# Twenty loads of a fused attention and gated-unit kernel, each cut into a 120-row and an 8-row transfer

## The chip, the cores and the metric

The kernel runs on one core of one Trainium2 chip. The metric is the device time of one execution in microseconds (us). Before the change three runs gave a median of 178.63 us (178.54 to 179.7). A further execution was recorded by the hardware profiler, and all views of the profile come from that one.

The core has five engines that run their own instruction streams side by side: TensorE (PE, matmuls; its weight loads are listed as PEld), VectorE (DVE), ScalarE (ACT), GpSimd (POOL) and SyncE (SP). SP computes nothing here: it issues the transfers between the chip's memory (HBM) and the on-chip memory (SBUF), which sixteen DMA engines carry out.

## The reference

Block-wise causal attention over 8 batches and 8 heads (576 positions, head size 64, blocks of 64 positions), whose output, with the heads side by side, goes through a gated linear unit with a causal convolution of five taps. All inputs and the output are float32.

```python
def _attn_ref(q, k, v):
    scores = (1.0 / np.sqrt(D)) * np.matmul(q, k.transpose(0, 1, 3, 2))
    scores = np.where(block_i >= block_j, scores, -1000000000.0)      # blocks of 64
    attn = np.exp(scores - np.max(scores, axis=-1, keepdims=True))
    attn = attn / (np.sum(attn, axis=-1, keepdims=True) + 1e-09)
    return np.matmul(attn, v)

def _moe_ref(x, w_val, conv_w, w_out):                # x: [8, 576, 512]
    for k in range(5):
        gate_pre += conv_w[k][None, None, :] * xp[:, k:k + S, :]
    gate = 1.0 / (1.0 + np.exp(-gate_pre))
    return gate * (x @ w_val) @ w_out
```

## The kernel before

The order of all work is written out by hand. A string, `PLAN` (lines 12 to 116), lists some 900 steps as `name/arguments/engine/banks`. The loop at the end (line 711) walks through it and calls the function of each step, which appends its instructions to the stream of the named engine. Each engine then runs its own steps in that order, and waits only where data or a buffer requires it. So the order on SP is the order in which the `S` steps stand in the plan.

The attention works in units. A unit `u` (0 to 15) is half a batch: four heads. Its q and k arrive through `lq(u, h)` and `lk(u, h)`, each with two halves `h`, 32 loads of q and 32 of k in all. One such load (`load_qk`, line 263) fills 128 partitions ("rows") of a staging buffer with 576 float32 numbers each: 64 groups of nine positions for each of two heads. There are three staging buffers each for q and for k, so a load waits until the buffer's old content has been used. `cd(u, i)` (line 351) then casts a unit's q (`i` = 0) or k (`i` = 1), both halves at once, to float16, on POOL, DVE or ACT. For the first unit `cds` does so half by half. `Tt` (line 388) transposes the result on PE, `Te` copies it back to SBUF as `qkT`, and `S` (scores), `E` (exponential, ACT), `A` (times v), `Nr`/`Nm` (normalization, DVE) and `X`/`Xe` (transpose into `xt`) follow for each pair of heads. v comes by `lv` (line 279) in 64 loads of 128 rows and four pieces of 256 bytes each, and is cast by `cv`; the last 64 positions of each batch come by `lvt`.

The gated unit then takes runs of 464 columns of `xt`: `C` (convolution on PE), `CS` (tanh on ACT), `V` (times `w_val`), `Ve` (gate times value into `gv`, DVE, line 653), and then `O` (times `w_out`), `Oe` (copy out) and `Od` (line 682, store, issued by SP).

The two weight matrices are loaded once, by `lwv` (line 291) and `lwo` (line 296), two loads each. One load fills 128 rows with two pieces of 512 float32 numbers. They borrow the memory of `gv` and of the output buffers `osb` as staging, and are cast by `cwv` and `cwo`.

All of these loads and stores are issued on SP's queue. Nearly every issue there carries a completion counter out of a ring of eight, and an issue waits until the transfer that last used its counter, eight issues earlier, has landed in full. At most eight transfers are therefore under way at a time. The profile's lines for these instructions are L265 (q and k), L281 (v), L287 (end of v), L292 and L297 (weights) and L683 (stores). Line 253 is the copy helper for DVE and POOL, line 251 that for ACT, line 144 the matmul helper and line 148 the transpose helper.

Of the kernel before, what the change touches and what calls it, by code (L numbers as in the profile page):

```python
# [119 lines left out]
def kernel(  # L120
# [37 lines left out]
    def consts(n, shape, dt, tag):  # L158
        return [const(shape, dt, f"{tag}_{i}") for i in range(n)]
# [56 lines left out]
    qks = [consts(3, [128, 2, 576], fp32, f"{n}s") for n in "qk"]  # L216
# [17 lines left out]
    w_val_st = gv[0:128, 0:4096].bitcast(fp32).rearrange("p (f n) -> p f n", f=4)  # L234
# [3 lines left out]
    w_out_st = osb_all[0:128, 0:2048].rearrange("p (f n) -> p f n", f=4)  # L238
# [5 lines left out]
    def rot(tiles, i):  # L244
        return tiles[i % len(tiles)]

    DMA = {"S": nc.sync, "A": nc.scalar}
# [12 lines left out]
        return f  # L260


    def load_qk(i, u, h, eng):
        b, w = divmod(u, 2)
        DMA[eng].dma_start(  # L265
            out=rot(qks[i], u)[0:128, h],
            in_=(q, k)[i][b, 4 * w + h:4 * w + h + 3:2, 0:576, 0:64].rearrange(
                "x (p n) d -> p x (n d)", n=9))

    @op  # L270
    def lq(u, h, eng="S", bank=None):
        load_qk(0, u, h, eng)

    @op
    def lk(u, h, eng="S", bank=None):
        load_qk(1, u, h, eng)
# [12 lines left out]

    @op  # L290
    def lwv(f, eng="S", bank=None):
        DMA[eng].dma_start(out=w_val_st[0:128, 2 * f:2 * f + 2],  # L292
                           in_=moe_w_val[256 * f:256 * f + 256].rearrange("(f p) n -> p f n", p=128))

    @op
    def lwo(f, eng="S", bank=None):
        DMA[eng].dma_start(out=w_out_st[0:128, 2 * f:2 * f + 2],  # L297
                           in_=moe_w_out[256 * f:256 * f + 256].rearrange("(f p) n -> p f n", p=128))

    @op  # L300
    def lcv(eng="S", bank=None):
# [409 lines left out]
    for word in PLAN.split():  # L711
        name, args, eng, bank = (word.split("/") + [""])[0:4]
        a = [int(i) for i in args.split(".") if i]
# [51 lines left out]
```

## Time and profile before

| | |
|---|---|
| runs shown, median | 178.63 us (178.54 to 179.7) |
| the profiled execution, its own time | 177.31 us |
| its span, from the first to the last instruction | 175.5 us |
| mean granted TensorE clock over the span | 0.968 |
| VectorE busy | 121.6 us (69%) |
| ScalarE busy | 144.8 us (82%) |
| GpSimd busy | 70.9 us (40%) |
| read from HBM, written to it | 30.42 MB, 9.44 MB |
| q and k loads, 288 KB each | 64 |
| v loads, 128 KB each | 64 and 8 |
| weight loads, 512 KB each | 4 |
| stores of 256 KB | 35 |

Times in the profile are counted from the first instruction of the span. An engine counts as busy while an instruction of it runs; SP's issues do not count. The ends of matmuls are modelled, so a busy PE is not necessarily at its best rate. In rows of the timeline the last bracket names how long the engine had been idle and what ended that; "issue" there means that the engine was waiting for nothing that the profile records.

### The profile page before, as it was taken

To read this page: it belongs to the slowest core of one execution; us is meant where nothing else is said; L and a number is where in the kernel's file an instruction comes from. 1 tells how busy PE (TensorE), PEld (TensorE's weight loads), DVE (VectorE), ACT (ScalarE), POOL (GpSimd) and SP (SyncE) were. 2 spreads that over 40 slices of the span, in tenths; PEclk is the share of its full clock that TensorE was granted. 3 is DMA by queue.
4 is the path that set the end of the run, shared out by engine and by line. 5 is a ranking of instruction groups with operands and counts; after the bars stand their busy time and mean duration, and the time that the engine had idled before them with its cause. 6 is when DMAs were issued, how large, how long until landed. Compare 5 with 4: busy or idle time off the path is not lost.

```text
span 175.5 us, 8114 instructions
## 1 busy us (share of the span) xinstructions
PE 165.6 (94%) x3498; PEld 99.6 (57%) x3498; DVE 121.6 (69%) x247; ACT 144.8 (82%) x179; POOL 70.9 (40%) x146
## 2 busy tenths in 40 slices
PE   6799899899999899899999999999999999999991
PEld 1456566456756465567556755665556665664540
DVE  2547998588769683999756998976698685545420
ACT  3799999889999699789889679988898878954562
POOL 5121875772552631486533643174546440100000
PEclk9855999999999999999999999999999999999998
DMA  4999899999999779998999969999987022103175
GB/s 141 306 364 280 234 241 392 327 232 252 238 301 262 132 185 287 334 292 241 311 327 246 304 197 259 290 302 222 322 253 213 4 97 86 63 4 120 38 296 209
DMA packets 53694, 40.38 MB, mean 230 GB/s; under 512 B 39701, under 2 KB 39957, under 8 KB 53658
## 3 DMA queue, kind: packets, MB, share of 16 engines
q1 hardware_dynamic: 53514, 39.74, 78.7%
q8 instruction: 27, 0.44, 1.1%
q10 hardware_dynamic: 144, 0.13, 0.2%
q14 instruction: 9, 0.07, 0.1%
HBM read 30.42 MB, written 9.44 MB: 227 GB/s over the span
## 4 chain that ended last, share of the span: by engine, by line
PE 80%; ACT 9%; DVE 3%; issue 3%; DMA 2%; SPq 0%; DVEq 0%; ACTq 0%
PE PS L144 72%; PE PS L148 8%; ACT pt L449 7%; DMA qs<-in_q_dram 2%; DVE gv L658 1%; ACT qkT L251 1%; DVE x L528 1%; DVE qkT L253 1%; DVE xt L253 0%; ACT q L251 0%; SPq L265 0%; ACT osb L251 0%; DVE rc L523 0%; ACT pt L488 0%; ACT late L251 0%
## 5 line engine op out<-in xcount | busy, mean ns | idle before, releaser
L449 ACT ACTIVATE pt<-PS 128x1024 f16<-128x1024 f32 (+1 forms) x102 | 93.8, 988 | 10.4 <-PE PS L144 8.8
L144 PE MATMUL PS<-qkT 64*128 64x64 f16 (+4 forms) x512 | 39.7, 257 | 2.3 <-issue 0.8
L144 PE MATMUL PS<-w_out,gv 128*128 128x512 f16 (+1 forms) x148 | 35.7, 374 | 0.2 <-DVE x L528 0.2
L144 PE MATMUL PS<-xt,w_val 128*128 128x464 f16 x160 | 35.7, 360 | 0.0
L658 DVE SCALAR_TENSOR_TENSOR gv<-th,PS 128x112 f16<-128x112 f32 (+4 forms) x64 | 26.2, 450 | 12.3 <-PE PS L144 6.0
L253 DVE COPY qkT<-PS 128x1152 f16<-128x1152 f16 (+1 forms) x22 | 29.1, 1326 | 8.1 <-PE PS L148 4.0
L144 PEld LDWEIGHTS <-pt 128*128 128x128 f16 (+1 forms) x960 | 27.9, 102 | 6.5 <-issue 1.8
L144 PE MATMUL PS<-v,pt 128*128 128x65 f16 (+1 forms) x896 | 31.1, 194 | 0.2 <-issue 0.2
L144 PEld LDWEIGHTS <-qkT 64*128 64x128 f16 x512 | 17.7, 96 | 18.6 <-issue 14.2
L640 ACT ACTIVATE th<-PS 128x928 f32<-128x928 f32 x20 | 17.8, 941 | 7.2 <-PE PS L144 7.1
L528 DVE TENSOR_TENSOR x<-PS,rc 128x512 f16<-128x512 f32 x32 | 22.1, 691 | 1.0
L144 PEld LDWEIGHTS <-w_val 128*128 128x128 f16 x160 | 13.9, 97 | 15.2 <-issue 3.6
L499 POOL MEMSET pt<- 64x256 f16 x32 | 10.9, 345 | 27.7 <-ACT pt L449 27.3
L144 PEld LDWEIGHTS <-gv 128*128 128x128 f16 x148 | 12.6, 97 | 13.5 <-issue 2.2
L253 POOL CAST k<-ks 128x1152 f16<-128x1152 f32 x12 | 13.8, 1148 | 11.9 <-DMA ks<-in_k_dram 6.0
L253 POOL CAST q<-qs 128x1152 f16<-128x1152 f32 x11 | 12.6, 1147 | 12.9 <-PE PS L144 6.1
L253 POOL CAST v<-vs 128x512 f16<-128x512 f32 x24 | 14.6, 618 | 6.7 <-DMA vs<-in_v_dram 5.1
L494 POOL MEMSET pt<- 64x256 f16 x32 | 10.0, 313 | 17.3 <-ACT pt L449 16.5
L253 DVE COPY xt<-PS 128x512 f16<-128x512 f16 (+1 forms) x30 | 11.6, 397 | 4.5 <-ACT th L640 2.3
L251 ACT COPY qkT<-PS 128x1152 f16<-128x1152 f16 (+1 forms) x16 | 14.2, 908 | 0.4 <-PE PS L148 0.4
L144 PE MATMUL PS<-xt,DG 32*32 32x464 f16 x800 | 13.0, 358 | 0.8 <-issue 0.7
L253 DVE COPY osb<-PS 128x512 f32<-128x512 f32 x17 | 11.6, 687 | 2.4 <-PE PS L144 1.7
(57 smaller groups left out, 135.3 us busy)
## 6 DMA issues: line engine op xcount, KB each, us to landing
ks<-in_k_dram SPq DMA_DIRECT2D x32, 288.0 KB, 5.0
qs<-in_q_dram SPq DMA_DIRECT2D x32, 288.0 KB, 5.5
out_dram<-osb SPq DMA_DIRECT2D x35, 256.0 KB, 4.3
vs<-in_v_dram SPq DMA_DIRECT2D x64, 128.0 KB, 5.1
vts<-in_v_dram SPq DMA_DIRECT2D x8, 128.0 KB, 5.0
osb<-in_moe_w_out_dram SPq DMA_DIRECT2D x2, 512.0 KB, 4.6
gv<-in_moe_w_val_dram SPq DMA_DIRECT2D x2, 512.0 KB, 5.7
out_dram<-late SPq DMA_DIRECT2D x1, 128.0 KB, 2.0
```

What stands on the lines that cost most here:

```text
L144: made.append(nc.tensor.matmul(out=out, lhsT=lhsT, rhs=rhs, start=start, stop=stop, skip_group_check=True))
L148: made.append(nc.tensor.transpose(out=out, in_=in_, identity=identity))
L251: i = nc.scalar.copy(out=out, in_=in_)
L253: i = (nc.vector if eng == "V" else nc.gpsimd).tensor_copy(out=out, in_=in_)
L449: made.append(nc.scalar.activation(out=o, in_=r, func=AF.Exp, bias=0.0, scale=0.125))
L494: nc.gpsimd.memset(rot(pts, p)[64:128, 0:2, 0:1024].rearrange("p h (t s) -> p h t s", t=2)[:, :, :, 0:64], 0.0)
L499: nc.gpsimd.memset(rot(pts, p)[64:128, 0:2, 640:1408].rearrange("p h (t s) -> p h t s", t=2)[:, :, :, 0:64], 0.0)
L528: made.append(nc.vector.tensor_tensor(out=rot(x16, p)[0:128].rearrange("p i h d -> p h i d"), in0=r[:, :, :, 0:64], in1=rot(rcs, p)[0:128] ...
L640: made.append(nc.scalar.activation(out=rot(ths, n)[0:128, 2 * i:2 * i + 2], in_=both(take("C", n, i))[:, :, 0:RUN], func=AF.Tanh, bias=0.0 ...
L658: made.append(nc.vector.scalar_tensor_tensor(out=gv[0:128, x, a - 4 * i:e - 4 * i], in0=rot(ths, n)[0:128, x, a - o:e - o], scalar=1.0, in ...
```

## The change

Twenty loads are each issued as two transfers, one of the first 120 rows and one of the last 8, one behind the other on the same queue. These are the four weight loads and sixteen of the 64 loads of q and k: q(1, 1), k(1, 1), k(2, 1) and q(3, 0), and then one of the four of each unit from 4 to 15 (k for odd units, q for even ones; half 0 for units 4, 5, 8, 9, 12, 13, half 1 for the others). The source and the destination of every byte stay as they are, and so do the plan and all instructions on the other four engines. SP issues twenty transfers more, and each of the twenty takes a counter of the ring of eight.

```diff
+    PARTED = {(0, 1, 1), (1, 1, 1), (1, 2, 1), (0, 3, 0)} | {(u % 2, u, u // 2 % 2) for u in range(4, 16)}
+
     def load_qk(i, u, h, eng):
         b, w = divmod(u, 2)
-        DMA[eng].dma_start(
-            out=rot(qks[i], u)[0:128, h],
-            in_=(q, k)[i][b, 4 * w + h:4 * w + h + 3:2, 0:576, 0:64].rearrange(
-                "x (p n) d -> p x (n d)", n=9))
+        src = (q, k)[i][b, 4 * w + h:4 * w + h + 3:2, 0:576, 0:64].rearrange(
+            "x (p n) d -> p x (n d)", n=9)
+        cuts = (0, 60, 64) if (i, u, h) in PARTED else (0, 64)
+        for a, e in zip(cuts, cuts[1:]):
+            DMA[eng].dma_start(out=rot(qks[i], u)[2 * a:2 * e, h], in_=src[a:e])
...
     def lwv(f, eng="S", bank=None):
-        DMA[eng].dma_start(out=w_val_st[0:128, 2 * f:2 * f + 2],
-                           in_=moe_w_val[256 * f:256 * f + 256].rearrange("(f p) n -> p f n", p=128))
+        src = moe_w_val[256 * f:256 * f + 256].rearrange("(f p) n -> p f n", p=128)
+        for rows in (slice(0, 120), slice(120, 128)):
+            DMA[eng].dma_start(out=w_val_st[rows, 2 * f:2 * f + 2], in_=src[rows])
```

`lwo` changes as `lwv` does, with `w_out_st` and `moe_w_out`.

More of the change, by code (lines that the diff above doesn't have):

```diff
@@ L291, in lwv @@
     def lwv(f, eng="S", bank=None):
-        DMA[eng].dma_start(out=w_val_st[0:128, 2 * f:2 * f + 2],
-                           in_=moe_w_val[256 * f:256 * f + 256].rearrange("(f p) n -> p f n", p=128))
+        src = moe_w_val[256 * f:256 * f + 256].rearrange("(f p) n -> p f n", p=128)
+        for rows in (slice(0, 120), slice(120, 128)):
+            DMA[eng].dma_start(out=w_val_st[rows, 2 * f:2 * f + 2], in_=src[rows])
     @op
     def lwo(f, eng="S", bank=None):
-        DMA[eng].dma_start(out=w_out_st[0:128, 2 * f:2 * f + 2],
-                           in_=moe_w_out[256 * f:256 * f + 256].rearrange("(f p) n -> p f n", p=128))
+        src = moe_w_out[256 * f:256 * f + 256].rearrange("(f p) n -> p f n", p=128)
+        for rows in (slice(0, 120), slice(120, 128)):
+            DMA[eng].dma_start(out=w_out_st[rows, 2 * f:2 * f + 2], in_=src[rows])
     @op
```

## The prediction

> **What bounds the kernel now.** I read the first page, then a table of busy time by stretch, then the waits of PE, SP's own timeline, and the waits of the casts that consume the loads. The page first.
>
> ```profile
> span 175.5 us, 8114 instructions
> PE 165.6 (94%) x3498; PEld 99.6 (57%) x3498; DVE 121.6 (69%) x247; ACT 144.8 (82%) x179; POOL 70.9 (40%) x146
> ...
> q1 hardware_dynamic: 53514, 39.74, 78.7%
> q8 instruction: 27, 0.44, 1.1%
> ...
> PE 80%; ACT 9%; DVE 3%; issue 3%; DMA 2%; SPq 0%; DVEq 0%; ACTq 0%
> ```
>
> PE is busy 94% of the span and carries 80% of the chain that ended last. The table of four stretches (start and end, length, then each engine's busy time, the granted clock, the mean busy share of the sixteen DMA engines and GB/s) says where PE is not full.
>
> ```profile
> 0.00:25.00 25.00, 21.50 (x339) 12.38 (x339) 15.70 (x29) 20.80 (x32) 10.90 (x34) 0.80 0.89 259
> 25.00:76.00 51.00, 48.27 (x1144) 29.51 (x1141) 38.66 (x81) 46.08 (x53) 25.58 (x51) 1.00 0.98 269
> 76.00:131.00 55.00, 54.98 (x1270) 33.60 (x1268) 43.80 (x85) 48.09 (x56) 25.68 (x44) 1.00 0.97 274
> 131.00:175.50 44.50, 40.81 (x763) 24.08 (x762) 23.47 (x56) 29.80 (x41) 8.70 (x19) 0.99 0.33 115
> ```
>
> From 25 to 76 us PE is idle for 51.00 - 48.27 = 2.73 us; from 76 to 131 it is idle for 0.02. So faster loads can win about 2.7 us in the second stretch and next to nothing in the third, where they can only lose. The DMA engines are at 0.98 and 0.97 in both, so the loads run close to their own limit beside PE.
>
> Three pauses of PE in the second stretch have no data as their cause. The waits of PE sum them up, the timeline places them, and a table cut at the points where PE resumes counts what lies between.
>
> ```profile
> PE PS L144 <- issue: 1.7, 3, 0.8
> ...
> 31.25 0.62 PE L144 MATMUL PS<-xt,DG 32*32 32x464 f16 x32 [0.71 <-issue]
> ...
> 59.29 0.42 PE L144 MATMUL PS<-qkT 64*128 64x64 f16 x6 [0.81 <-issue]
> ...
> 64.80 0.39 PE L144 MATMUL PS<-v,pt 128*128 128x65 f16 x7 [0.15 <-issue]
> ...
> 31.25:59.29 28.04, 27.05 (x639) 16.58 (x640) 21.52 (x45) 25.03 (x29) 15.21 (x26) 1.00 1.02 256
> 59.29:64.80 5.51, 5.35 (x129) 3.14 (x128) 3.79 (x8) 5.19 (x6) 2.32 (x4) 1.00 0.69 156
> ```
>
> Between the first two resumptions PE ran 639 + 640 = 1279 instructions, between the next two 129 + 128 = 257: five times 256, and once. Queue q8 moved 0.44 MB in 27 packets, 16.3 KB each. Divided by PE's 3498 + 3498 instructions that is 63 bytes for one, or 256 instructions a packet. So q8 brings PE's own program in blocks of 256, and PE stood still three times (0.71 + 0.81 + 0.15 = 1.67 us) because a block came late. That program travels over the same DMA engines as the loads. One packet takes 1.1% x 16 x 175.5 / 27 = 1.14 us of one engine. In the second stretch PE runs 1144 + 1141 instructions, about nine blocks or 10.2 us. If one engine carries them all, it has 10 us of extra work in 51 us in which the sixteen are 0.98 busy on average, so it must be the last to finish most loads.
>
> **The change part by part.** First the cost: twenty more issues on SP. SP's timeline (start, length, count) and the spread of the issues' lengths (minimum, median, maximum in ns):
>
> ```profile
> 56.20 3.35 SPq L265 DMA_DIRECT2D qs<-in_q_dram  x1
> 59.65 2.19 SPq L281 DMA_DIRECT2D vs<-in_v_dram  x4
> 61.89 2.14 SPq L265 DMA_DIRECT2D ks<-in_k_dram  x1
> 64.12 0.54 SPq L281 DMA_DIRECT2D vs<-in_v_dram  x1
> 64.71 0.54 SPq L265 DMA_DIRECT2D qs<-in_q_dram  x1
> ...
> 131.81 37.55 SPq L683 DMA_DIRECT2D out_dram<-osb  x12
> ...
> L265 SPq DMA_DIRECT2D ks<-in_k_dram x32: 534/604/2137, 0.7 to 127.0; - x32
> L265 SPq DMA_DIRECT2D qs<-in_q_dram x32: 534/600/3352, 1.4 to 126.4; - x32
> ...
> SPq L265 <- DMA osb<-in_moe_w_out_dram: 1.6, 1, 1.6
> ```
>
> An issue has a median of 0.60 us, so twenty cost 12 us of SP in its first 131 us. A small piece has no row. The nearest is the shortest q or k issue, 0.53, and the longest, 3.35, was not its own work; I take 0.60. Whether a later issue makes the loads later depends on the stalls it meets: the issue at 56.20 took 2.75 us more than the median, the one at 61.89 1.54 more, and a q load waited 1.6 us for the counter of a weight load. These are times in which the DMA engines held SP up. A delay of 0.60 that runs into such a stall shortens it and is gone. The sixteen q and k splits lie several microseconds apart, so I count the issues at nothing while those stalls stand, and at 0.60 us for each load that is awaited where they don't. The ring of eight counters shrinks in bytes, above all behind the weights, whose eight pieces fill it; that is again a place where the engines are backed up.
>
> Second the relief.
>
> ```profile
> ks<-in_k_dram SPq DMA_DIRECT2D x32, 288.0 KB, 5.0
> ...
> gv<-in_moe_w_val_dram SPq DMA_DIRECT2D x2, 512.0 KB, 5.7
> ```
>
> 128 rows on sixteen engines are 8 rows each: 18 KB of a q or k load, 32 KB of a weight load. 120 rows are 15 times 8, so the large piece can fill fifteen engines exactly as before and leave the sixteenth out, and the last 8 rows go to whichever engines take the small piece. An engine moved 39.74 MB / 16 = 2.48 MB in 78.7% of 175.5 = 138 us, 18 bytes a nanosecond. The engine left out is thus spared 1.0 us at each q or k split and 1.8 at each weight split: 16 x 1.0 + 4 x 1.8 = 23 us, against 27 x 1.14 = 31 us of PE's program. No view shows single engines, so two things are taken on trust: that one engine is left out, and that it is the one that fetches. [...] No run here shows that yet, nor which engine fetches.
>
> If so, 4 x 1.8 us of relief stand right before the pause that ends at 31.25, and 1.0 us or more before each of the others, while the pauses are 0.71, 0.81 and 0.15 long. I take them as gone: 1.67 us. Bounds: nothing if the fetch isn't what queues, 1.67 if it is.
>
> Third, a load that PE waits for in the same stretch (DVE, then PE; and the landing time of the one q load issued at 64.71):
>
> ```profile
> 66.67 0.42 DVE L253 CAST v<-vs 128x512 f16<-128x512 f32 x1
> 70.08 0.76 DVE L253 CAST q<-qs 128x1152 f16<-128x1152 f32 x1 [2.99 <-issue]
> 70.76 1.30 DVE L658 SCALAR_TENSOR_TENSOR gv<-th,PS 128x228 f16<-128x228 f32 x4
> ...
> 70.90 0.44 PE L148 MATMUL PS<-ident,q 64*128 64x64 f16 x18 [0.56 <-DVE q L253]
> ...
> DMA to landing us min/median/max: 5.3/5.3/5.3
> ```
>
> The load lands at 64.71 + 5.3 = 70.0, DVE has been idle since 67.1 and casts at once, and PE waits 0.56 us for it. This load stands behind the stalls of 2.75 and 1.54 us. If the late engine caused half of them, it is issued 2 us earlier, less the 0.60 of the split beside it: more than the 0.56 that PE needs. I count 0.4, between nothing and 0.56, since DVE's next steps move up only as far as their own inputs do.
>
> Sum: 1.67 + 0.4 = 2.1 us, inside the 2.73 of idle time. In the first stretch I count nothing.
>
> ```profile
> 12.00:25.00 13.00, 12.07 (x235) 7.96 (x233) 11.10 (x13) 12.96 (x19) 6.86 (x13) 0.79 0.98 257
> ...
> 9.54 1.14 POOL L253 CAST q<-qs 128x1152 f16<-128x1152 f32 x1 [4.08 <-DMA qs<-in_q_dram]
> ```
>
> ACT is busy 12.96 of 13.00 us from 12 to 25, so earlier loads win nothing. The cast at 9.54 waits for q(1, 0) and q(1, 1), which is split: its small piece is issued 0.60 later, and that is the price if nothing behind it has room.
>
> **The rivals.** *The gain is given back.* From 76 us on, PE is full and several casts start the moment their load lands, with PE right behind them:
>
> ```profile
> 116.58 1.15 POOL L253 CAST k<-ks 128x1152 f16<-128x1152 f32 x1 [0.87 <-DMA ks<-in_k_dram]
> 125.50 1.15 POOL L253 CAST q<-qs 128x1152 f16<-128x1152 f32 x1 [0.73 <-DMA qs<-in_q_dram]
> ...
> 126.70 0.44 PE L148 MATMUL PS<-ident,q 64*128 64x64 f16 x18
> ...
> 82.99 0.30 PEld L148 LDWEIGHTS <-q 64*128 64x128 f16 x13 [0.23 <-POOL q L253]
> ```
>
> The cast at 125.50 ends at 126.65 and PE uses it at 126.70. If PE arrives 2 us earlier and these loads don't, PE waits there, and the time is what it was, 178.6, or 0.5 less. Against it: the loads wait for buffers that a faster PE frees earlier, and the spared engine helps these loads too.
>
> *Slower: the wrong engine is spared.* Then every split costs its issue and no stall gets shorter. It decides at the loads that PE awaits, at 70.1, 82, 116.6 and 125.5 us; each is one 0.60 later, 2.4 us in all: 181.0. Were the extra rows put on the engine that fetches, the three pauses would grow too, doubled to 182.7. For it: no row names the engine. [...] Against it: the pauses and stalls need a backed-up engine, and the spared bytes go to engines without program to carry.
>
> *The pieces do nothing at all*, since every transfer is off PE's chain (DMA has 2% of it, at the start). That is the first rival's time with another cause, and is counted there.
>
> **How the numbers follow.** The profiled execution took 177.31 us, 1.8 more than its span; the median of the runs is 178.63, 1.3 above it. 177.31 - 2.1 = 175.2, and moved to the median 176.5. A measurement of this kernel tells about 1% (1.8 us) from no change. Chances: the forecast 0.55, of which 0.45 beyond 1% (a gain above 1.8) and 0.10 within; the gain given back 0.20, within 1%; slower 0.25, of which 0.02 within. So faster 0.45, same 0.32, slower 0.23. The forecast's own range is 175.3 (2.73 of idle time all won, and the 0.60 of the first stretch's cast with its sign turned) to 177.5 (the pauses alone, two thirds of them). Up to the slower rival it runs to 181.2, leaving out some 0.05 below and 0.12 above.
>
> **What would show it.** Right: no wait of PE for "issue" in the waits; the issues near 56 and 62 us back at 0.6; DVE's q cast near 70 us with less idle before it; more busy time of PE in the 25 to 76 stretch. Wrong: pauses of the same length or longer at counts of 256, SP's issues with no stall left between 25 and 131 us, or PE waiting for POOL's casts beyond 76 us, where it waits for none now but by tenths.

## The result, and the profile after

The changed kernel took 189.89 us (median of 4 runs, 188.92 to 190.73) against 178.78 us (178.54 to 179.7) for the kernel before on the same chip: 1.062 times as long, 95% interval 1.056 to 1.069. The forecast was 176.5 with a range up to 181.2. The profiled execution took 188.92 us.

The first page of the profile after:

```profile
span 187.1 us, 8146 instructions
PE 169.8 (91%) x3498; PEld 99.9 (53%) x3498; DVE 121.0 (65%) x247; ACT 146.0 (78%) x179; POOL 71.2 (38%) x146
...
q1 hardware_dynamic: 53590, 39.74, 79.0%
q8 instruction: 27, 0.44, 1.1%
...
PE 51%; DMA 23%; SPq 10%; DVE 6%; issue 5%; ACT 2%; POOL 1%; DVEq 0%; POOLq 0%; ACTq 0%
```

The same bytes and the same matmuls, but in the chain that ended last transfers have taken over part of what was PE's: PE has 51% of it, before 80%, DMA 23%, before 2%, and SP's issues 10%, before 0%. The granted clock is not the cause: its mean was 0.991, before 0.968. The stretches of the forecast's table, with the last one up to the new end:

```profile
0.00:25.00 25.00, 21.75 (x288) 11.06 (x290) 14.17 (x27) 19.66 (x30) 8.31 (x29) 1.00 0.85 230
25.00:76.00 51.00, 44.60 (x1070) 27.03 (x1067) 33.45 (x71) 41.59 (x47) 24.74 (x49) 0.97 0.99 229
76.00:131.00 55.00, 52.20 (x1181) 32.09 (x1168) 41.98 (x81) 46.06 (x54) 23.74 (x41) 1.00 0.97 267
131.00:187.10 56.10, 51.28 (x982) 29.74 (x977) 31.38 (x69) 38.73 (x51) 14.36 (x28) 1.00 0.46 148
```

From 25 to 76 us PE is idle for 6.4 us instead of 2.73, from 76 to 131 for 2.8 instead of 0.02. The DMA engines are busy for 0.99 of the second stretch as before (0.98), and yet move 229 GB/s instead of 269: they work as long for less. To see where PE falls behind, count its matmuls from the start to 76 and to 131 us, first before, then after:

```profile
0.00:76.00 76.00, 69.77 (x1475) 41.89 (x1476) 54.36 (x109) 66.88 (x84) 36.48 (x84) 0.93 0.95 266
0.00:131.00 131.00, 124.74 (x2738) 75.49 (x2740) 98.16 (x192) 114.97 (x139) 62.16 (x127) 0.96 0.96 269
```

```profile
0.00:76.00 76.00, 66.35 (x1356) 38.08 (x1356) 47.62 (x97) 61.24 (x76) 33.05 (x78) 0.98 0.94 229
0.00:131.00 131.00, 118.56 (x2523) 70.17 (x2524) 89.60 (x178) 107.30 (x129) 56.79 (x118) 0.99 0.95 245
```

PE is 51 matmuls behind at 25 us (288 against 339), 119 at 76 and 215 at 131. Before, PE ran (2738 - 1475) / 55 = 23 a microsecond there, so 215 are about 9.4 us. The loss has no single place: it starts in the first stretch and grows as long as there are loads.

The waits of POOL, whose casts are the first to use most loads (total, times, longest in us), before and after:

```profile
POOL k L253 <- DMA ks<-in_k_dram: 6.0, 5, 2.2
...
POOL q L253 <- DMA qs<-in_q_dram: 5.5, 4, 4.1
POOL v L253 <- DMA vs<-in_v_dram: 5.1, 6, 1.7
```

```profile
POOL k L253 <- DMA ks<-in_k_dram: 12.3, 6, 3.2
...
POOL v L253 <- DMA vs<-in_v_dram: 7.8, 6, 3.0
POOL q L253 <- DMA qs<-in_q_dram: 7.5, 3, 5.5
```

PE's own waits, and the pause for its program in its timeline:

```profile
PE PS L144 <- issue: 2.3, 1, 2.3
PE PS L148 <- POOL k L253: 2.1, 2, 1.3
```

```profile
33.77 0.42 PE L144 MATMUL PS<-xt,DG 32*32 32x464 f16 x15
36.53 1.57 PE L144 MATMUL PS<-xt,DG 32*32 32x464 f16 x65 [2.34 <-issue]
```

Of the three pauses before (0.71, 0.81, 0.15) the first has grown to 2.34 us, in the same convolution right behind the weights; the others are gone, but PE now waits for data instead. The records of queue q8 bear out that such a pause waits for a block of PE's program: a packet of 16 KB had come in 1.4 to 1.6 us before PE resumed, at the pause here and at the three before. A piece of the chain of waits shows how data come late (start, length, what): a k load takes 4.16 us to land, POOL casts it 0.9 us later, and PE's transposes start as the cast ends.

```profile
121.83 4.16 DMA ks<-in_k_dram
125.98 0.76 issue
...
126.87 1.16 POOL k L253
...
128.07 0.81 PE PS L148 x44
```

SP's timeline after, two lines with a split load (x2 is the pair of pieces; the loads of q and k are issued by line 271 in the changed kernel):

```profile
49.34 1.64 SPq L271 DMA_DIRECT2D qs<-in_q_dram  x2
...
59.20 1.72 SPq L271 DMA_DIRECT2D ks<-in_k_dram  x2
```

A pair holds SP for 1.64 to 1.72 us, where a whole load's median was 0.60. Taken apart in the trace's records, the 120-row piece has a median of 0.92 us and the 8-row piece of 0.72 (16 of each); the eight weight pieces have 0.33, against 0.49 for the four whole loads. The records of the counters show how often a transfer raises its counter as it lands: a whole load 16 times, a 120-row piece 15 times, an 8-row piece of q or k 4 times and one of the weights 8 times. (Each of these pieces raises it once more within 0.5 us of the end of its issue, long before the others, which begin at least 2.7 us after the start of the issue; that one is left out of all counts here.) In what follows one completion is read as one engine whose share has landed, so that a 120-row piece takes 15 of the sixteen engines and gives each 8 rows. This is an inference from the counts: no record names an engine.

### The profile page after: what moved, and what is told of

Its sections match the earlier page's. It is cut to its first block, busy times and chain, and to the rows that moved or that the text cites. A ratio compares the mean times of both kernels' runs of the same rounds, so it can differ in the third digit from the quotient of the medians.

```text
span 187.1 us, 8146 instructions
## 1 busy us (share of the span) xinstructions
PE 169.8 (91%) x3498; PEld 99.9 (53%) x3498; DVE 121.0 (65%) x247; ACT 146.0 (78%) x179; POOL 71.2 (38%) x146
## 4 chain that ended last, share of the span: by engine, by line
PE 51%; DMA 23%; SPq 10%; DVE 6%; issue 5%; ACT 2%; POOL 1%; DVEq 0%; POOLq 0%; ACTq 0%
PE PS L144 47%; DMA ks<-in_k_dram 9%; DMA qs<-in_q_dram 6%; SPq L271 6%; DMA vs<-in_v_dram 5%; PE PS L148 4%; DMA vts<-in_v_dram 3%; SPq L284 2%; DVE x L533 1%; DVE qkT L253 1%; SPq L688 1%; ACT pt L454 1%; DVE gv L663 1%; SPq L290 1%; POOL k L253 1%
## 5 line engine op out<-in xcount | busy, mean ns | idle before, releaser
L144 PE MATMUL PS<-xt,w_val 128*128 128x464 f16 x160 | 36.9, 369 | 0.0
L144 PE MATMUL PS<-v,pt 128*128 128x65 f16 (+1 forms) x896 | 31.4, 194 | 3.2 <-DVE gv L663 1.2
L144 PEld LDWEIGHTS <-pt 128*128 128x128 f16 (+1 forms) x960 | 28.1, 102 | 10.1 <-issue 4.1
L253 POOL CAST v<-vs 128x512 f16<-128x512 f32 x24 | 15.5, 650 | 11.0 <-DMA vs<-in_v_dram 7.8
L499 POOL MEMSET pt<- 64x256 f16 x32 | 10.2, 323 | 12.0 <-ACT pt L454 11.1
```

The lines of the kernel that those rows point to most:

```text
L144: made.append(nc.tensor.matmul(out=out, lhsT=lhsT, rhs=rhs, start=start, stop=stop, skip_group_check=True))
L253: i = (nc.vector if eng == "V" else nc.gpsimd).tensor_copy(out=out, in_=in_)
L499: nc.gpsimd.memset(rot(pts, p)[64:128, 0:2, 0:1024].rearrange("p h (t s) -> p h t s", t=2)[:, :, :, 0:64], 0.0)
```

## The experiments

Each ratio is to the kernel before on the same chip, with a 95% interval.

**Parts of the change.** Only the weights cut, only the twelve late loads (units 4 to 15), only the four early ones:

```diff
-    PARTED = {(0, 1, 1), (1, 1, 1), (1, 2, 1), (0, 3, 0)} | {(u % 2, u, u // 2 % 2) for u in range(4, 16)}
+    PARTED = set()                                                   # weights only
+    PARTED = {(u % 2, u, u // 2 % 2) for u in range(4, 16)}          # late only, weights whole
+    PARTED = {(0, 1, 1), (1, 1, 1), (1, 2, 1), (0, 3, 0)}            # early only, weights whole
```

> The four weight loads are cut into 120 and 8 rows, q and k are loaded whole. Theory A (transfers of 120 rows move slower, because fifteen engines get in each other's way where sixteen do not): in the changed kernel 225 GB/s were moved from 25 to 39 us at a full DMA share, against 325 from 22 to 32 us before, and PE's work behind the weights slipped by some 4.3 us more; so about 183 us, with the same 225 GB/s behind the weights. Theory B (the time is SP's own: more issues, and more counters of the ring of eight taken): eight weight pieces were issued in 0.33 us each, 2.7 us in all against 2.0 for four whole ones, so at most 1 us for the issues and 2 for the counters, 180 to 181 us, with GB/s as before.

> Only the twelve q and k loads of units 4 to 15 are cut into 120 and 8 rows; the weights and the first four are whole. In the changed kernel PE's work slipped by some 4.5 us between the transposes of unit 4 and the end. If the parts add up: about 183 us. If most of that slip was a late effect of the weights: under 181. If the cuts help once the weights are whole, as was forecast: under 178.

> Only the four q and k loads of units 1 to 3 are cut. In the changed kernel PE stood 2.6 us behind by the transposes of unit 3. If the parts add up: about 181 us. If that delay is absorbed later by whole weights: 179 to 180.

Measured: weights 1.022 (1.014 to 1.031), late 1.024 (1.016 to 1.031), early 1.018 (1.009 to 1.027). Of 178.8 us that makes 182.8, 183.0 and 182.0 us: the weights nearer to theory A than to B, the late loads as they must be if the parts add up, the early ones above what was expected. Together they are 6.4%, against 6.2% for the whole change. So none of the three parts wins anything, and within the intervals none hides behind another.

**The same number of transfers, cut by columns.** All twenty loads as two transfers of all 128 rows, each with half of the numbers of a row:

```diff
-        cuts = (0, 60, 64) if (i, u, h) in PARTED else (0, 64)
+        cuts = (0, 288, 576) if (i, u, h) in PARTED else (0, 576)
         for a, e in zip(cuts, cuts[1:]):
-            DMA[eng].dma_start(out=rot(qks[i], u)[2 * a:2 * e, h], in_=src[a:e])
+            DMA[eng].dma_start(out=rot(qks[i], u)[0:128, h, a:e], in_=src[:, :, a:e])
...
-        for rows in (slice(0, 120), slice(120, 128)):
-            DMA[eng].dma_start(out=w_val_st[rows, 2 * f:2 * f + 2], in_=src[rows])
+        for c in (0, 1):
+            DMA[eng].dma_start(out=w_val_st[0:128, 2 * f + c], in_=src[:, c])
```

> The same twenty loads are each issued as two transfers, but cut in columns: each piece has all 128 rows, the weights in pieces of 512 numbers, q and k in pieces of 288. So there are as many issues and as many counters as in the changed kernel, but every piece can go to all sixteen engines evenly. Theory A: most of the 11 us are gone, 179 to 182 us, and GB/s behind the weights as before the change. Theory B: it stays near 188 to 190.

Measured: 1.024 (1.014 to 1.034), as theory A has it, with 315 GB/s from 25 to 39 us against 321 before. Twenty cuts that leave all rows together cost 2.4%; the other 3.8% come with the cut by rows. Not all of the 3.8% need be the transfers: a split of q or k by rows holds SP for 1.64 us, one by columns for 1.21. And not all of the 2.4% need be issues and counters: the packets of the cut q and k loads are also halved here, and move 1152 bytes in 51 ns instead of 2304 in 93.

**The weights alone, by columns and in halves of 64 rows.**

```diff
-        for rows in (slice(0, 120), slice(120, 128)):
+        for rows in (slice(0, 64), slice(64, 128)):                  # q and k whole
```

> Only the four weight loads are cut, each into 64 and 64 rows, q and k are whole. As many transfers as in the run with the weights alone cut 120 and 8 (+2.2%). Theory A, the loss comes from transfers that fifteen or eight engines carry: both halves should be counted by sixteen completions, the stretch from 25 to 39 us moves more than 300 GB/s again, ratio 1.00 to 1.01. Theory B, any second transfer of a weight load costs it, by its issue and its counter: ratio 1.017 to 1.03. Theory C, a cut by rows is what is slow, whatever the number of engines: 1.02 or more, with the run cut by columns at 1.00 to 1.01.

> Only the four weight loads are cut, each into two transfers of all 128 rows with one piece of 512 numbers, q and k are whole. Theory A (narrow transfers are slow): 1.00 to 1.01, as with 64 and 64 rows. Theory B (a second transfer costs, whatever its shape): 1.017 to 1.03. Four issues of 0.43 us by themselves are 1.7 us of SP, which is 1.0% if all of it is on the path.

Measured: 64 rows 1.017 (1.012 to 1.022), columns 1.004 (1.000 to 1.009). Both make eight transfers of the same size, and both are counted by sixteen completions. Theory A fell, since the 64-row halves have sixteen completions as a whole load has, and theory B with the column cut. C is what is left, its 1.02 a little high: a cut by rows is what costs. (An issue is also longer, 0.61 us for 64 rows against 0.43 for a column, but the DMA engines are full in both runs, at 1.07 and 1.06 below, so they don't wait for SP.) The stretch from 23 to 37 us, in which the weights move, shows how. Its last two columns are the busy share of the engines and GB/s; before, after, weights 120 and 8, 64 rows, columns:

```profile
23.00:37.00 14.00, 13.12 (x309) 7.69 (x308) 10.69 (x20) 12.93 (x15) 9.76 (x22) 1.00 1.07 332
```

```profile
23.00:37.00 14.00, 9.61 (x281) 6.84 (x280) 8.88 (x18) 10.83 (x11) 6.69 (x18) 1.00 0.97 216
```

```profile
23.00:37.00 14.00, 10.44 (x272) 6.45 (x267) 8.13 (x16) 10.99 (x13) 5.21 (x16) 1.00 0.96 222
```

```profile
23.00:37.00 14.00, 12.03 (x312) 7.70 (x310) 9.30 (x20) 12.45 (x14) 6.33 (x18) 1.00 1.07 254
```

```profile
23.00:37.00 14.00, 13.84 (x342) 8.77 (x339) 12.51 (x21) 13.72 (x15) 10.58 (x23) 1.00 1.06 322
```

Divide GB/s by sixteen times the share: an engine that is busy moves 332 / (16 x 1.07) = 19.4 GB/s before, 13.9 after, 14.5 with the weights in 120 and 8 rows, 14.8 in 64 rows, and 19.0 by columns. The records of single packets say the same. A packet of 2048 bytes of the weights takes 84 ns (median of 1024) before and by columns, 141 after, 142 with 120 and 8 and with 64 rows. Loads that nobody cut suffer with them: while the weights move, the packets of q and k, which are loaded whole in these runs, take 93 ns before and by columns, but 174 next to pieces of 120 and 8 rows and 154 next to 64.

**Is it the number of engines or the rows that each gets?** The weights alone in 104 and 24 rows, and in 117 and 11. The numbers of engines are an estimate from the counts above, all of which divide the rows evenly (128 by 16, 120 by 15, 8 by 8 or 4): read the same way, 104 rows are thirteen shares of 8 and 117 rows thirteen of 9. If fewer engines make each packet slower (theory N), both take some 140 ns a packet:

```diff
-        for rows in (slice(0, 120), slice(120, 128)):
+        for rows in (slice(0, 104), slice(104, 128)):                # 13 x 8 rows, 12 x 2
+        for rows in (slice(0, 117), slice(117, 128)):                # 13 x 9 rows, 11 x 1
```

> Only the four weight loads are cut, into 104 and 24 rows, q and k whole: thirteen engines with 8 rows each and twelve with 2. [...] The kernel: 1.015 to 1.035.

> Only the four weight loads are cut, into 117 and 11 rows, q and k whole: thirteen engines again, but with 9 rows each, and eleven with 1. [...] Theory N: about 140 ns as with thirteen engines of 8 rows, and the same time as that run.

```profile
23.00:37.00 14.00, 11.46 (x283) 7.15 (x280) 7.81 (x17) 11.30 (x13) 5.33 (x17) 0.88 0.96 229
```

```profile
23.00:37.00 14.00, 12.23 (x294) 7.24 (x292) 9.21 (x19) 11.89 (x14) 6.52 (x17) 1.00 0.97 264
```

The packet takes 136 ns with 104 rows and 98 with 117, by the estimate on as many engines; a busy engine moves 14.9 and 17.0 GB/s. So by the estimate the number of engines is not what slows these packets, against theory N. Two runs shown below agree: the weights in 126 rows (fourteen shares of 9) have 84 ns, in 88 rows (eleven of 8) 133. The kernels, however, came out alike, 1.012 (1.006 to 1.019), below what was expected of the first, and 1.012 (1.006 to 1.018): the faster packets of the second didn't show in its time. The whole loads of q and k between the pieces stay slow in both, with 154 and 141 ns a packet. And if the pieces take thirteen and twelve, and thirteen and eleven, of sixteen engines, at least nine and eight of them carry rows of both: 10 rows of each weight load by the estimate (8 + 2 and 9 + 1), where a whole load gives each 8.

What slows the packets of the weights is not shown. It is not the size of the share alone either: a whole load also comes to 8 rows for each of sixteen engines, and has 84 ns where 104 and 120 rows have 136 to 142. Which rows an engine gets, and which engine, is not recorded in the trace, and why q and k stay slow next to 117 rows is left open.

A try to drive this further, the weights in pieces of 16 rows:

```diff
-        for rows in (slice(0, 120), slice(120, 128)):
+        for rows in (slice(r, r + 16) for r in range(0, 128, 16)):
```

> Only the weights are cut, each load into eight transfers of 16 rows, 28 transfers more in all; the number to read is the time of a packet of 2048 bytes between 25 and 39 us, not the kernel's. So far: 84 ns where a transfer spans all 128 rows (whole, or cut by columns), 141 to 144 ns for 120 rows on fifteen engines and for 64 rows on sixteen. [...] Theory N, any transfer that doesn't span all 128 rows is slow alike: about 144 ns again. The kernel's time: 1.03 or more by either, by the issues alone 28 x 0.3 to 0.6 us of SP.

Measured: 1.073 (1.065 to 1.080), and a packet of 84 ns in the median, a quarter of them over 127. The time is in the range that was expected, the packet is far from the 144 ns of theory N. The busy share from 25 to 39 us says why:

```profile
25.00:39.00 14.00, 7.52 (x224) 5.14 (x221) 6.10 (x13) 9.21 (x11) 3.30 (x11) 0.82 0.45 121
```

The engines are 0.45 busy. SP can't issue such small pieces fast enough to load them, at 0.42 us each, so the run tells nothing about what full engines would do with them.

**q and k: the second issue, and the 120-row piece.** Late loads with the second piece left out, and whole loads with a second issue that moves next to nothing:

```diff
-        for a, e in zip(cuts, cuts[1:]):
+        for a, e in list(zip(cuts, cuts[1:]))[:1]:                   # late loads only
```

```diff
+    spare = const([128, 64], fp32, "spare")
...
+    extra = list(range(16))
...
-        for a, e in zip(cuts, cuts[1:]):
-            DMA[eng].dma_start(out=rot(qks[i], u)[2 * a:2 * e, h], in_=src[a:e])
+        DMA[eng].dma_start(out=rot(qks[i], u)[0:128, h], in_=src)
+        if (i, u, h) in PARTED:
+            at = 8 * extra.pop()
+            DMA[eng].dma_start(out=spare[at:at + 8], in_=src[60:64, :, 0:64])
```

> The twelve q and k loads of units 4 to 15 move their first 120 rows only; their last 8 rows are left out, so the kernel computes with old numbers there and SP issues no transfer more than before. Weights and early loads are whole. Theory A, the 120-row transfer is itself slower (it was issued in 0.92 us against 0.60, and moved 225 GB/s against 325 behind the weights): most of the loss of the run with late q and k cut (+2.4%) stays, ratio 1.015 to 1.024. Theory B, the loss is the second issue of 0.72 us and the counter it takes: the ratio falls to 1.00 to 1.008.

> All twenty loads are whole as before; behind each of the sixteen q and k loads that the change cuts, one more transfer of 8 rows and 64 numbers goes into a spare buffer that nobody reads. It adds the second issue and its counter and next to no bytes. Theory I, the issues and counters carry the loss of the q and k part (late 2.4%, early 1.8%): ratio 1.025 to 1.04. Theory S, they carry what the column cut showed without its weights (2.4 - 0.4 = 2.0%), and the rest is the slower transfer of 120 rows: 1.012 to 1.025. Theory P, the slow transfer carries nearly all: 1.00 to 1.01.

Measured: 120 rows alone 1.017 (1.010 to 1.024), theory A: most of the late loads' 2.4% stays with no issue added. The packets of q and k say why. Of those that begin between 40 and 131 us, 13% take over 120 ns before and 16% with the extra issues, but 22% with 120 rows alone, 22% with the late loads cut and 21% in the changed kernel. Whole and extra 1.010 (1.005 to 1.015), at the upper edge of theory P and below S: sixteen second issues cost 1.0%, where the q and k splits cost 1.8 + 2.4 = 4.2%. SP's timeline of this run shows the extra issue behind its whole load:

```profile
51.44 0.56 SPq L272 DMA_DIRECT2D ks<-in_k_dram  x1
52.04 0.69 SPq L275 DMA_DIRECT2D spare<-in_k_dram  x1
```

Its sixteen extra issues hold SP for 16 x 0.68 = 10.9 us, and still it loses only 1.8. The records of SP's issues up to the last load suggest why. Before, 20 of them last over 1.1 us, 21.2 us in all beyond 0.60 each; with the extra issues 14, 11.1 beyond. So the stalls gave back 10.1 of 10.9 us, as the forecast had it. In the changed kernel the q and k splits add 16 x (0.92 + 0.72 - 0.60) = 16.6 us, and the stalls shrink only from 21.2 to 15.7: they gave back 5.5 of it.

**Fewer issues.** Both halves of q, and of k, of units 4 to 15 by one transfer of 576 KB, at the place of the first half:

```diff
+    merged = set()
...
+        if u >= 4:
+            if (u, i) in merged:
+                return
+            merged.add((u, i))
+            DMA[eng].dma_start(
+                out=rot(qks[i], u)[0:128, 0:2],
+                in_=(q, k)[i][b, 4 * w:4 * w + 4, 0:576, 0:64].rearrange(
+                    "(x h) (p n) d -> p x h (n d)", h=2, n=9))
+            return
```

> The other way round: the two halves of q and of k of units 4 to 15 are loaded by one transfer of 576 KB, at the place of the first half in the queue, 24 issues fewer than before. Theory A (issues and counters are what the loads pay): twenty column cuts cost 2.4%, 4.2 us, 0.2 us each, so 24 fewer could give up to 5 us, of which PE's idle time from 25 to 76 us lets 1.5 to 2.7 through: ratio 0.985 to 0.992. Theory B (the order and the bytes in flight decide): the second half now stands ahead of v loads that are wanted sooner, ratio 1.00 to 1.015.

Measured: 1.005 (1.001 to 1.010), theory B. Twenty-four issues less, in this order, gain nothing; what they would be worth in an order that doesn't put half of each load earlier wasn't tried. No run here was faster than the kernel before.

**Which engine fetches PE's program.** The same twenty loads with fewer engines for the large piece: 112 and 16 rows, then 88 and 40. Fourteen completions count a 112-row piece; eleven engines for 88 rows, of 8 each, are the estimate by even shares (the lines of q and k; the weights are named beside them):

```diff
-        cuts = (0, 60, 64) if (i, u, h) in PARTED else (0, 64)
+        cuts = (0, 56, 64) if (i, u, h) in PARTED else (0, 64)       # weights 126 and 2
+        cuts = (0, 44, 64) if (i, u, h) in PARTED else (0, 64)       # weights 88 and 40
```

> [...] Time: by either, as slow as the change or up to 2% slower (a spared engine's rows are spread on others): ratio 1.05 to 1.09, with 1.04 to 1.06 if the pauses go.

> [...] Time: eleven engines carry 8 rows each and ten 4 more, 12 where a whole load gives each 8, so the pieces take half as long again: ratio 1.05 to 1.10.

Measured: 1.056 (1.047 to 1.064) and 1.083 (1.075 to 1.092), inside the ranges of both. That ten engines carry 4 rows more for each load in the second, 12 in all, was the author's estimate; no record shows which engines carry both pieces. PE has no wait for "issue" in either, but it has none in the run with the weights in 64 rows either, where sixteen completions count each half. PE waits for casts of loads in all three (up to 2.3, 3.2 and 1.3 us at a time), so its program may be there in time for that reason, and the absence of such a wait tells nothing about relief here. What remains is the lag of the last completion. In the trace of the changed kernel, with a block of PE's program moving from 60.73 to 62.27 us:

```
issued   rows  completions  last but one  last
59.20    120   15           63.23         65.61
60.18      8    4           63.23         63.77
```

One of the fifteen completions of the 120-row piece is 2.4 us behind the other fourteen, and all four of the 8-row piece, issued later, come before it. With fourteen engines the large pieces still lag now and then (issued at 47.68, fourteen completions: 52.49, then 53.88). The engine that falls behind is therefore, with a completion read as an engine, one of those that the split still loads, not the one that it spares. That it is the engine that fetches is inferred from the times; no run spared it without slowing all others, and what its relief would bring wasn't tried.

## Why the prediction was wrong

**What it had right.** PE's program comes by an engine that carries loads too, as far as the late completions tell; the 120-row piece leaves one of sixteen out, going by its 15 completions; the pieces of the weights hold up the issues behind them (a q or k load waits 1.9 us for one, before 1.6); and a second issue that meets a stall mostly vanishes in it (10.1 of 10.9 us in the run with extra issues).

**"The large piece can fill fifteen engines exactly as before."** This is the step that failed. A busy engine moved 13.9 GB/s instead of 19.4 behind the weights. The four weight loads, last landed at 31.4 us before and at 30.8 when cut by columns, landed at 36.5 when cut 120 and 8 with all else whole. The runs with the weights alone cost 0.4% (landed at 30.8, columns), 1.2% (34.8, shares of 9 rows), 1.7% (35.3, 64 rows), 2.2% (36.5, 120 and 8) and 1.2% (36.6, thirteen shares of 8 rows). So every late landing cost more than the early one, but the last run breaks the order, and the landing is not the whole price. The forecast counted bytes for each engine, at one rate of 18 bytes a nanosecond for every shape.

**"An issue has a median of 0.60 us ... I take 0.60", and nothing for those that meet a stall.** The small piece took 0.72 us, and the large one grew from 0.60 to 0.92, so a split added 1.04 us, not 0.60, and there were not enough stalls to take that: the stalls, which the slower transfers keep alive, gave back 5.5 of 16.6 us. That transfers and queue together make the 4.2% of q and k follows from the runs; how it divides was only bounded: 1.0% for second issues alone, 1.7% for twelve 120-row pieces without one (of this some may be the 0.32 us by which their own issue is longer).

**"I take them as gone: 1.67 us."** The pauses did not go; the one behind the weights grew to 2.34. The forecast left open which engine fetches, and the late completion among the fifteen speaks against it, since the engine that lags is not the one left out.

**"In the first stretch I count nothing."** The four early splits alone cost 1.8%. POOL's first cast of q, at 9.54 us before, comes at 11.33 in that run: the price named there, 0.60, was right in kind and too small.

**The rivals.** "The wrong engine is spared" had the sign and the signature (casts on POOL that wait for loads, PE behind them), and a price of 2.4 us for four awaited loads. The loss was over 11. The rival counted late issues alone; it named neither the slower transfers nor the longer issues. And every load was late by more than one issue, in a queue where each issue starts when the one before it is done (the 120-row piece issued at 49.34 us took 0.90, and its 8-row piece followed at 50.29): by 131 us SP had made 164 issues where 160 had been made before, though nineteen of the 164 were added ones. A cut by rows costs even in two equal halves: 1.7% for halves of 64 rows in place of the whole weights.

## What to carry to other kernels

A load that spans all 128 rows should be cut by columns, if it must be cut at all: 0.4% against 1.2 to 2.2% by rows in two for the same weights. Before a transfer's shape is changed, ask what its rows do to the rate (98 ns a packet with 117 rows, 136 with 104), and read GB/s divided by the busy share: engines that are nearly as busy and move less are the sign (0.97 and 216 GB/s after, 1.07 and 332 before). A stall in SP's queue hid a second issue as long as the transfers that fill the queue kept their speed (10.1 of 10.9 us), and not where they slowed (5.5 of 16.6).

## What was not expected of the hardware

A packet of 2048 bytes took 84 ns when the transfer spanned 128 rows, 136 to 142 ns with the weights in 104, in 120 or in 64 rows, and 98 ns in 117. Whole loads of q and k in flight beside weights cut by rows slowed from 93 ns a packet of 2304 bytes to between 141 and 174. An issue of a q or k load on SP took 0.60 us for 128 rows, 0.92 for 120 and 0.72 for 8 rows, so the time of an issue doesn't follow the bytes; the weights' pieces took 0.33.
